# Induced-set attention with a maxout MLP: four block copies on GpSimd, one fp32 matmul later, another table of departures

## The chip, the cores and the metric

One Trainium2 chip, one core of it. The metric is the device time of one execution in microseconds (us); of several runs the median is taken.

## The reference

There are four batches of 12544 tokens with 128 channels, 32 inducing vectors, and a maxout MLP with 1024 hidden columns. Cut to what matters:

```python
def mab(q, kv):                       # scale = 1 / sqrt(128)
    s = scale * (q @ kv.transpose(0, 2, 1))
    a = np.exp(s - s.max(-1, keepdims=True))
    a /= a.sum(-1, keepdims=True) + 1e-09
    return a @ kv
h = mab(I, x)                         # 32 summary rows per batch
x = mab(x, h).reshape(B * N, 128)     # every token attends to the 32 rows
return np.maximum(x @ w1, x @ w2) @ w_out
```

## The kernel before

Each batch is 98 chunks of 128 tokens. The kernel works in two passes per batch. The first pass makes the 32 rows h: scores against the inducing vectors, exponentials, sums over tokens. The second pass never forms the attention output. As max(a, b) = a + max(0, b - a), the kernel applies the weights to h first: `hwd` is h times (w2 - w1), `m1` is h times w1 times w_out. For a token with exponentials e, the unnormalised result is relu(e hwd) w_out + e m1, and the division by the sum of e comes last, at the output.

The tokens of the second pass are cut into blocks of up to 16 chunks, four quarters of up to four chunks; a quarter's exponentials lie on 32 of the 128 partitions. These steps work on them:

- **Scores** (`stage`, L614): a column-tiled burst on TensorE of one block; ScalarE takes the exponentials (L633). Several blocks can follow one another in a burst.
- **Row phase** (`phase`, L1028): four row-tiled jobs side by side, each filling one PSUM bank. A job makes hidden columns from e and `hwd`, or opens an output group with e times `m1`. ScalarE (L1044) or VectorE (L1047) takes the relu of a bank.
- **Finals** (`final_one`, L840): matmuls of 128x128 that multiply relu tiles with w_out into an output group. VectorE scales a finished group (L867) and SyncE's queue stores it (L895).

In the first and last block some groups are "full": they aren't opened in a row phase. `linear_last` closes them (L817) with e on all 128 partitions times `m1bd`, a 128x4x128 tile that holds the q-th 32 rows of m1 in slot q and zeros elsewhere. GpSimd zeroes the tile once, at the start (L221).

The first pass of batch b + 1 is threaded into the second pass of batch b. `pool_accum` (column bursts, L384 and L403) sums over tokens; VectorE adds the parts into the tile `hacc` (L415 and L417). From `hacc` runs a chain of small steps. `small_rep` multiplies `hacc` by the fp32 tile `repd` (L429), so that h's sums stand four times over the partitions; VectorE takes the reciprocal (L432) and scales (L434). `small_h` transposes the result (L442, copied at L444). `small_hwd` makes `hwd` (L505, evicted at L508 and L511). `small_m1` makes m1 (L518), and VectorE casts it out of PSUM (L525 and L529), in batches 0 and 3 also blocks of it into `m1bd`, one instruction for each 32 partitions, ahead of m1 itself.

The order of all instructions is fixed while the program is built. A planner (`Clock`) keeps an estimated time for TensorE, ScalarE, VectorE and each PSUM bank, and at each step picks a row phase, a column burst, a final or a small step. `ready` says when a small step may go: `small_rep` as soon as the estimate says that `hacc` is written (`esrr`). The table `DEV` lists steps at which the planner departs from its own rule: 1 prefers finals, 2 a phase, 3 suppresses column work, 4 asks for column work early. On the chip semaphores keep the order right: an instruction whose input is late waits, and everything behind it on its engine waits too.

Of the kernel before, what the change touches and what calls it, by code (L numbers as in the profile page):

```python
# [16 lines left out]
INF = 1e9  # L17
# [85 lines left out]
def kernel(  # L103
# [9 lines left out]
    nc = tc.nc  # L113
    B, N, C = x.shape
# [27 lines left out]
    def bank(shape, dtype=F32, only=None):  # L142
        i = min(range(8), key=lambda j: ck.bank[j]) if only is None else only
        uid[0] += 1
        return i, psum.tile(shape, dtype, name=f"ps{uid[0]}", tag=f"bank{i}", bufs=1)
# [46 lines left out]
    m1bd = consts.tile([128, 4, C], F16, name="m1bd")  # L192
# [5 lines left out]
    with tc.manual_schedule(engines={ET.PE, ET.DVE, ET.Activation, ET.Pool, ET.SP}):  # L198
# [80 lines left out]
        def p1_esum(i):  # L279
            n = parts[0][i][1]  # L280
            et, ready = st[0]["et", i]
            ck.wait(ready, "p1")
            j = 0
            for m in pieces(n):
                nc.tensor.matmul(
                    out=st[0]["eps"][0 : m * M, 0:1],
                    lhsT=et[:, j : j + m, :].rearrange("p k m -> p (k m)"),
                    rhs=ones16[:, 0:1],
                    start=(summed["E"] == 0),
                    stop=(summed["E"] + m == K),  # L290
                    skip_group_check=True,
                )
                j += m
                summed["E"] += m
            st[0]["endE"] = ck.run(0.03 * len(pieces(n)))

        def p1_hsum(i, lo=0, hi=P1):
            n = parts[0][i][1]
            et, ready = st[0]["et", i]
            ck.wait(ready, "p1")  # L300
            for j in range(lo, min(hi, n)):
                nc.tensor.matmul(  # L302
                    out=st[0]["hps"][:, 0:M],
                    lhsT=xn_at[0, i][:, j, :],
                    rhs=et[:, j, :],
                    start=(summed["H"] == 0),
                    stop=(summed["H"] == K - 1),
                )
                summed["H"] += 1
            st[0]["end"] = ck.run(0.029 * (min(hi, n) - lo))  # L310
# [175 lines left out]
        def small_sums():  # L486
            es, ready = st[0]["es"]
            ps = st[0]["eps"]
            ck.wait(ready, "p1")
            nc.tensor.matmul(out=ps[:, 2:3], lhsT=rep32, rhs=es, start=True, stop=True, skip_group_check=True)  # L490
            end = ck.run(0.11)
            st[0]["rs"] = smp.tile([128, 1], F32, name="rs_0", tag="rs_")
            st[0]["rw"] = smp.tile([128, 1], F32, name="rw_0", tag="rw_")
            nc.vector.reciprocal(out=st[0]["rs"], in_=ps[:, 2:3])
            nc.vector.tensor_scalar(out=st[0]["rw"], in0=st[0]["rs"], scalar1=1.0 / scale, scalar2=None, op0=ALU.mult)
            ck.bank[st[0]["eb"]] = st[0]["rsr"] = ck.on_dve(end, 0.34)
# [18 lines left out]
        def small_m1(b):  # L515
            bi, ps = bank([128, 512])
            ck.wait(max(ck.bank[bi], st[b]["hT4r"]), "p1")
            nc.tensor.matmul(out=ps[:, 0:128], lhsT=st[b]["hT4"], rhs=w1out, start=True, stop=True)  # L518
            end = ck.run(0.06)
            m1 = smp.tile([128, C], F16, name=f"m1_{b}", tag="m1")  # L520
            bd = {0: [0], B - 1: [0, 1, 2, 3]}.get(b, [])
            outs = [(m1bd[32 * q : 32 * (q + 1), q, :], slice(32 * q, 32 * (q + 1))) for q in bd]
            for o, r in outs + [(m1, slice(0, 128))]:
                if b == 0:
                    nc.vector.tensor_scalar(  # L525
                        out=o, in0=ps[r, 0:128], scalar1=st[0]["rw"][r, :], scalar2=None, op0=ALU.mult
                    )
                else:
                    nc.vector.tensor_copy(out=o, in_=ps[r, 0:128])  # L529
                ck.bank[bi] = ck.on_dve(end, 0.2)  # L530
            st[b]["m1"] = m1
            st[b]["m1r"] = ck.bank[bi]

# [386 lines left out]
        def want_linear():  # L920
# [31 lines left out]
        }  # L952
        LIMIT = -16

# [107 lines left out]
        for b in range(1, B):  # L1062
            base = DONE0[b - 1]
            t_first, t_step = (6, 2.2) if b == 1 else (-6, 3.4)
            for u in range(NU):
                if b == 1:
                    s, turn, acc = 25 + 5 * u, 45 + 1.5 * u, 55 + 2 * u
                else:
                    s = turn = 13 + 8.2 * u
                    acc = s + 12  # L1070
                at(base + int(s), pool_scores, b, u)
                at(base + int(turn), pool_turn, b, u)
                if u % 2:
                    at(base + int(acc), pool_accum, b, u)
            s, end = int(s), base + int(acc)
            at(base + s + 2, pool_rest, b)
            at(end, small_rep, b)
            at(end, small_h, b)
            at(end, small_hwd, b)
            at(end, small_m1, b)  # L1080
            for j in range(14):
                at(base + int(t_first + t_step * j), transpose_x_dma, b, j)
# [8 lines left out]
        def ready(f, a):  # L1091

            if f in (weights_1, weights_1b):
                return True
            d = st[a[0]]
            now = ck.pe
            if f is pool_scores and a[1] >= NEU and ("eT", a[1] - NEU) not in d:
                return False
            if f is pool_turn and a[1] >= NEU and ("sum", a[1] - NEU) not in d:
                return False  # L1100
            if f is pool_scores:
                return d.get(("T", (U * a[1] + U - 1) // (P1 // 2)), INF) + (8.0 if a[0] == 1 else 10.0) <= now
            if f is pool_rest:
                return d.get(("T", 13), INF) + 6.0 <= now
            if f is pool_turn:
                return d.get(("eu", a[1]), (0, INF))[1] <= now
            if f is pool_accum:
                return d.get(("eT", a[1]), (0, INF))[1] + (9.5 if a[0] == 1 else 11.5) <= now and (a[1] < NU - 1 or "et" in d)
            if f is small_rep:
                return d.get("esrr", INF) <= now  # L1110
            if f is small_h:
                return d.get("haccr", INF) <= now
            if f in (small_hwd, small_m1):
                if f is small_m1 and a[0] == 0 and w_of["w1out"] > now:
                    return False
                return d.get("hT4r", INF) <= now
            return True

        COL = (pool_scores, pool_accum)
        FULL = (pool_rest, small_rep, small_h, small_hwd, small_m1)  # L1120

        def side_work():
# [83 lines left out]
        while state["g"] < len(groups) or held:  # L1206
# [19 lines left out]
            now = tp <= ck.pe + early or tp <= tf and tf > ck.pe  # L1226
            if how == 1 and tf < INF:
                now = False
            if how == 2 and tp <= ck.pe + 0.2:
                now = True  # L1230
# [47 lines left out]
```

## Time and profile before

| | |
|---|---|
| runs | 326.05, 326.20, 543.13 us; median 326.2 us |
| profiled execution | 325.93 us, span 324.1 us, granted TensorE clock 1.0 |
| TensorE matmuls | 317.5 us busy (98%), 5404 instructions |
| TensorE weight loads | 241.2 us (74%) |
| VectorE | 283.4 us (87%), 512 instructions |
| ScalarE | 280.1 us (86%), 558 instructions |
| GpSimd | 28.0 us (9%), 56 instructions |
| memory traffic | 167 GB/s over the span |

The span runs from the first to the last instruction of the profiled execution; its own time has 1.8 us more around it. PE is TensorE, DVE is VectorE, ACT is ScalarE, POOL is GpSimd, SP is SyncE. A row of the timeline gives the start, the duration, the engine, the line, the operation, the tiles (output <- inputs), the shapes and a count when equal instructions were merged; in brackets stands the idle time before it and what ended it. Matmuls overlap: their durations include the pipeline, so the distance between two starts tells more than a duration does. A row of the busy times in stretches gives the stretch, its length, and then the busy time of PE, PEld (weight loads), DVE, ACT and POOL.

### The profile page before, as it was taken

What the parts mean: (1) busy time and instruction counts of PE and PEld (TensorE: products, weight loads), DVE (VectorE), ACT (ScalarE), POOL (GpSimd) and SP (SyncE); (2) the same over time, 40 slices, a digit from 0 to 9 for tenths busy, and PEclk for the clock granted to TensorE, in tenths of its full rate; (3) what the DMA queues carried; (4) which work ended last, traced back from release to release, by engine and by line L of the source; (5) the groups of instructions that cost most, each with busy time, mean ns of one, the idle gap of its engine ahead of it and who ended that gap; (6) DMA issues with size and microseconds to landing.
All of it is one profiled execution on the core that took longest, in us unless ns stands there. A gap on an engine that the chain in (4) does not pass through costs nothing.

```text
span 324.1 us, 12585 instructions
## 1 busy us (share of the span) xinstructions
PE 317.5 (98%) x5404; PEld 241.2 (74%) x5404; DVE 283.4 (87%) x512; ACT 280.1 (86%) x558; POOL 28.0 (9%) x56
## 2 busy tenths in 40 slices
PE   7899999999999999999999999999999999999996
PEld 3786777777767777777777777777777777777786
DVE  2479999988989998999989989988989999999974
ACT  4679899998878999999988999998879999999860
POOL 7460000000450000000040000000000000000000
DMA  8999999965779999984279999783421322223233
GB/s 205 207 202 213 215 223 196 237 136 134 232 161 242 225 247 210 192 188 121 101 150 243 219 254 217 163 204 107 117 99 67 115 86 81 82 90 127 84 114 115
DMA packets 71895, 53.65 MB, mean 166 GB/s; under 512 B 52352, under 2 KB 57376, under 8 KB 71840
## 3 DMA queue, kind: packets, MB, share of 16 engines
q1 hardware_dynamic: 65232, 38.57, 48.6%
q0 software_dynamic: 6464, 14.22, 22.8%
q8 instruction: 42, 0.69, 0.8%
q14 instruction: 13, 0.11, 0.1%
q10 hardware_dynamic: 144, 0.07, 0.1%
HBM read 28.33 MB, written 25.69 MB: 167 GB/s over the span
## 4 chain that ended last, share of the span: by engine, by line
PE 93%; DMA 3%; ACT 1%; POOL 1%; DVE 1%; issue 1%; POOLq 0%; DVEq 0%; ACTq 0%
PE ps L840 61%; PE ps L1028 22%; DMA xn<-in_x_dram 3%; PE ps L614 2%; PE ps L384 2%; PE ps L328 1%; PE ps L234 1%; PE ps L673 1%; PE ps L257 1%; ACT relu L1044 1%; PE ps L302 1%; PE ps L797 0%; PE ps L429 0%; PE ps L505 0%; POOL xn L166 0%
## 5 line engine op out<-in xcount | busy, mean ns | idle before, releaser
L1044 ACT ACTIVATE relu<-ps 128x512 f16<-128x512 f32 x462 | 244.2, 605 | 25.0 <-PE ps L1028 16.6
L1047 DVE TENSOR_SCALAR relu<-ps 128x512 f16<-128x512 f32 x322 | 206.0, 683 | 16.0 <-PE ps L1028 14.5
L840 PE MATMUL ps<-woutp,relu 128*128 128x128 f16 x3136 | 217.5, 220 | 0.0
L840 PEld LDWEIGHTS <-relu 128*128 128x128 f16 x3136 | 176.6, 98 | 39.3 <-issue 29.0
L1028 PE MATMUL ps<-e,hwd 32*128 32x512 f16 (+2 forms) x888 | 88.6, 358 | 0.3 <-ACT e L633 0.3
L867 DVE TENSOR_TENSOR o<-ps,rp 128x512 f32<-128x512 f32 (+3 forms) x108 | 68.5, 634 | 6.3 <-PE ps L840 3.4
L1028 PEld LDWEIGHTS <-hwd 32*128 32x128 f16 x888 | 24.6, 91 | 21.2 <-issue 1.1
L1028 PE MATMUL ps<-m,e 32*128 32x128 f16 x381 | 38.9, 217 | 0.0
L1028 PEld LDWEIGHTS <-e 32*128 32x128 f16 x381 | 21.2, 92 | 3.2 <-issue 0.7
L166 POOL DMA_DIRECT2D xn<-in_x_dram x33 | 18.2, 563 | 6.2 <-DMA xn<-in_x_dram 3.8
L339 ACT ACTIVATE eu<-ps 128x512 f16<-128x512 f32 x18 | 10.9, 615 | 0.1
L633 ACT ACTIVATE e<-ps 128x512 f16<-128x512 f32 (+2 forms) x21 | 10.5, 571 | 0.2 <-PE ps L614 0.2
L245 DVE COPY xT<-ps 128x512 f16<-128x512 f16 (+3 forms) x12 | 5.6, 484 | 5.7 <-PE ps L234 5.2
L234 PE MATMUL ps<-identity,xn 128*128 128x128 f16 x98 | 8.1, 221 | 1.3 <-DMA xn<-in_x_dram 0.8
L614 PE MATMUL ps<-xT,hT 128*32 128x512 f16 (+3 forms) x114 | 8.4, 361 | 0.0
L248 ACT COPY xT<-ps 128x896 f16<-128x896 f16 (+3 forms) x9 | 5.4, 622 | 3.2 <-PE ps L234 3.1
L234 PEld LDWEIGHTS <-xn 128*128 128x128 f16 x98 | 5.7, 98 | 2.7 <-DMA xn<-in_x_dram 1.4
L328 PE MATMUL ps<-xT,inducingT 128*32 128x512 f16 x72 | 6.3, 384 | 0.0
L164 POOL COPY pace<-hacc 128x1 f32<-128x1 f32 x2 | 0.4, 183 | 68.5 <-DVE hacc L417 68.5
L273 ACT ACTIVATE et<-ps 128x224 f16<-128x224 f32 (+3 forms) x11 | 4.1, 407 | 1.9 <-PE ps L257 1.8
L614 PEld LDWEIGHTS <-hT 128*32 128x32 f16 x114 | 2.8, 94 | 3.6 <-issue 2.4
L384 PE MATMUL ps<-xn,eT 128*32 128x128 f16 x288 | 5.5, 220 | 0.0
(94 smaller groups left out, 105.1 us busy)
## 6 DMA issues: line engine op xcount, KB each, us to landing
out_dram<-o SPq DMA_DIRECT2D x85, 256.0 KB, 2.5
xn<-in_x_dram POOLq DMA_DIRECT2D x24, 448.0 KB, 11.7
out_dram<-o SPq DMA_DIRECT2D x20, 128.0 KB, 2.0
xn<-in_moe_w_dram POOLq DMA_DIRECT2D x4, 256.0 KB, 3.9
xn<-in_x_dram POOLq DMA_DIRECT2D x3, 224.0 KB, 8.8
xT<-xn SPq DMA_TRANSPOSE x42, 3.9
xf<-in_x_dram SPq DMA_DIRECT2D x1, 512.0 KB, 3.6
xf<-in_x_dram SPq DMA_DIRECT2D x1, 384.0 KB, 4.0
```

Source lines behind the costliest of these rows:

```text
L166: nc.gpsimd.dma_start(out=xn_at[b, i][lo:hi, 0:n, :], in_=xr[b, lo:hi, k0 : k0 + n, :])
L234: nc.tensor.transpose(ps[:, j, :], xn_at[0, i][:, g + j, :], identity16)
L328: nc.tensor.matmul(out=ps[32 * g : 32 * (g + 1), :], lhsT=inducingT, rhs=xT_tiles[b % 2][:, U * u + 4 * g : U * u + 4 * (g + 1), :], start ...
L339: nc.scalar.activation(out=eu, in_=ps, func=AF.Exp, scale=scale, accum_out=st[b]["es"][:, u : u + 1])
L384: nc.tensor.matmul(out=ps[32 * g : 32 * (g + 1), 0:128], lhsT=eT[:, j, 32 * g : 32 * (g + 1)], rhs=xn_of(b, U * v + 4 * g + j), start=(j = ...
L614: nc.tensor.matmul(out=ps[32 * q : 32 * (q + 1), 128 * t : 128 * (t + n)], lhsT=hq, rhs=xT[:, c : c + n, :], start=True, stop=True, tile_p ...
L633: nc.scalar.activation(out=blk.e2[:, lo:hi], in_=ps[:, lo:hi], func=AF.Exp, scale=st[0]["rs"] if blk.b == 0 else scale,)
L840: nc.tensor.matmul(out=g.ps[:, 128 * c : 128 * (c + 1)], lhsT=g.blk.relu[q][:, 128 * (jb * w4 + t) : 128 * (jb * w4 + t + 1)], rhs=woutp[: ...
L867: nc.vector.tensor_mul(osb[:, 0:n, :], g.ps[:, 0 : n * C].rearrange("p (s c) -> p s c", s=n), rp)
L1028: nc.tensor.matmul(**seq[i])
L1044: nc.scalar.activation(out=dst, in_=src, func=AF.Relu)
L1047: nc.vector.tensor_scalar(out=dst, in0=src, scalar1=0.0, scalar2=None, op0=ALU.max)
```

## The change

It has three parts. In batch 3, `small_m1` casts m1 from PSUM first, and the four blocks of `m1bd` are then copied by GpSimd from m1 in SBUF; VectorE's four casts from PSUM are gone. Batch 0 keeps its one block on VectorE. In the planner, `small_rep` may go only 0.3 us (by the planner's estimate) after `hacc`. And the table of departures has other entries: 674 and 1517 go; 650, 659, 1467, 1486, 1522, 1604, 1613 and 1614 come. Lines behind 531 move down by five in the changed kernel (L840 becomes L845, L1028 becomes L1033, L817 becomes L822).

```diff
-            bd = {0: [0], B - 1: [0, 1, 2, 3]}.get(b, [])
-            outs = [(m1bd[32 * q : 32 * (q + 1), q, :], slice(32 * q, 32 * (q + 1))) for q in bd]
-            for o, r in outs + [(m1, slice(0, 128))]:
+            outs = [(m1, slice(0, 128))]
+            if b == 0:
+                outs.insert(0, (m1bd[0:32, 0, :], slice(0, 32)))
+            for o, r in outs:
...
                 ck.bank[bi] = ck.on_dve(end, 0.2)
+            if b == B - 1:
+                for q in range(4):
+                    r = slice(32 * q, 32 * (q + 1))
+                    nc.gpsimd.tensor_copy(out=m1bd[r, q, :], in_=m1[r, :])
...
-            579: 4, 580: 1, 584: 1, 587: 2, 616: 2, 638: 1, 646: 2, 658: 1, 674: 4, 685: 1, 688: 2, 690: 1,
+            579: 4, 580: 1, 584: 1, 587: 2, 616: 2, 638: 1, 646: 2, 650: 2, 658: 1, 659: 1, 685: 1, 688: 2,
...
-            1, 1492: 1, 1496: 1, 1507: 1, 1517: 1, 1521: 1, 1547: 1, 1557: 1, 1558: 3, 1564: 1, 1569: 1,
+            3, 1407: 4, 1409: 1, 1413: 3, 1420: 1, 1434: 1, 1442: 1, 1451: 4, 1454: 1, 1461: 2, 1467: 2,
+            1476: 3, 1480: 1, 1486: 1, 1492: 1, 1496: 1, 1507: 1, 1521: 1, 1522: 2, 1547: 1, 1557: 1, 1558:
+            3, 1564: 1, 1569: 1, 1596: 1, 1604: 2, 1613: 4, 1614: 1, 1639: 4, 1680: 1, 1682: 1, 1696: 1,
...
             if f is small_rep:
-                return d.get("esrr", INF) <= now
+                return d.get("esrr", INF) + 0.3 <= now
```

18 rows, old and new, of the table DEV are left out of this document.

## The prediction

> **What bounds the kernel now.** I read four views in this order: busy times and the chain that ended last, both on the profile page; TensorE's waits between 26 and 310 us; the busy times in stretches; the timeline around the lines that the change touches.
>
> ```profile
> PE 317.5 (98%) x5404; PEld 241.2 (74%) x5404; DVE 283.4 (87%) x512; ACT 280.1 (86%) x558; POOL 28.0 (9%) x56
> PE 93%; DMA 3%; ACT 1%; POOL 1%; DVE 1%; issue 1%; POOLq 0%; DVEq 0%; ACTq 0%
> PE ps L1028 <- ACT e L633: 0.3, 1, 0.3
> core 0: us, PE busy (x) PEld busy (x) DVE busy (x) ACT busy (x) POOL busy (x), PEclk, DMA share, GB/s
> 243.00:248.00 5.00, 5.00 (x90) 3.88 (x87) 4.40 (x10) 4.55 (x10) 0.00 (x0) 1.00 0.14 52
> 243.00:310.00 67.00, 67.00 (x1103) 51.41 (x1101) 63.23 (x109) 61.80 (x120) 0.00 (x0) 1.00 0.25 92
> ```
>
> TensorE is busy 98% of the span and carries 93% of the chain. The third row is the whole answer for its waits from 26 to 310 us: 0.3 us, once. But a busy share can hide short stops, because overlapping matmuls cover the gap between two starts; so below I work with starts. In the last stretch, which the new order rewrites most, VectorE is busy 63.23 of 67.00 us and ScalarE 61.80. They empty the banks that TensorE fills, and have 4 to 5 us of slack between them and TensorE. So VectorE's work matters only if its delay uses up this slack; time that is freed there is worth nothing by itself.
>
> **Part 1: batch 3's m1.** Four VectorE casts from PSUM go, the cast of m1 itself comes first, and four GpSimd copies follow it.
>
> ```profile
> 243.15 1.19 DVE L529 CAST m1bd<-ps 32x128 f16<-32x128 f32 x4 [0.72 <-PE ps L518]
> 244.35 0.29 DVE L529 CAST m<-ps 128x128 f16<-128x128 f32 x1
> L164 POOL COPY pace<-hacc 128x1 f32<-128x1 f32 x2 | 0.4, 183 | 68.5 <-DVE hacc L417 68.5
> L546 POOL TENSOR_TENSOR w<-xn,xn 128x512 f16<-128x512 f32 x2 | 2.5, 1268 | 4.1 <-DMA xn<-in_moe_w_dram 4.1
> 162.73 4.01 POOL L166 DMA_DIRECT2D xn<-in_x_dram  x7 [0.36 <-PE ps L429]
> 317.89 0.39 PE L817 MATMUL ps<-m1bd,e 128*128 128x128 f16 x4
> ```
>
> VectorE gets 1.19 us back, and m1 is ready 1.19 us earlier. TensorE had no wait there, so I cost this at nothing; the cover is its own dense stream. No SBUF copy of 32x128 by GpSimd is in the trace. It lies between 0.18 us (the 128x1 copy) and 1.27 us (the two-input 128x512 subtraction); I take 0.25, near the copy, since it has a single input and a quarter of the columns. That makes 1.0 us for four (bounds 0.7 to 5.1), ending near 244.5, or at worst 248.6. Their reader in the last block starts at 317.89, so some 70 us hide them, and its new wait on GpSimd is long met. Nothing stands behind the copies in GpSimd's queue: its last transfers were issued by 166.74. Cost: 0.
>
> **Part 2: the fp32 matmul (L429) later.** It reads the sum hacc, which VectorE writes at L417. Per batch, the rows from the work before to the work after:
>
> ```profile
> L429 PEld LDWEIGHTS ps<-hacc,repd x6: 186/188/191, 89.9 to 238.3; 128*128 128x128 f32 x6
> 89.52 0.34 PE L840 MATMUL ps<-woutp,relu 128*128 128x128 f16 x3
> 89.53 0.29 DVE L417 TENSOR_TENSOR hacc<-ps,hacc 128x129 f32<-128x129 f32 x1
> 89.97 0.46 PE L429 MATMUL ps<-hacc,repd 128*128 128x129 f32 x2
> 90.27 1.06 PE L840 MATMUL ps<-woutp,relu 128*128 128x128 f16 x16
> 161.35 0.73 PE L840 MATMUL ps<-woutp,relu 128*128 128x128 f16 x10
> 161.76 0.29 DVE L417 TENSOR_TENSOR hacc<-ps,hacc 128x129 f32<-128x129 f32 x1
> 162.20 0.46 PE L429 MATMUL ps<-hacc,repd 128*128 128x129 f32 x2
> 237.74 0.29 DVE L417 TENSOR_TENSOR hacc<-ps,hacc 128x129 f32<-128x129 f32 x1 [0.16 <-PE ps L403]
> 237.92 0.34 PE L840 MATMUL ps<-woutp,relu 128*128 128x128 f16 x3
> 238.06 1.29 DVE L1047 TENSOR_SCALAR relu<-ps 128x512 f16<-128x512 f32 x2
> 238.18 0.46 PE L429 MATMUL ps<-hacc,repd 128*128 128x129 f32 x2
> 239.26 0.16 DVE L432 RECIPROCAL rec<-ps 128x1 f32<-128x1 f32 x1
> 239.46 0.35 DVE L434 TENSOR_SCALAR h<-ps,rec 128x128 f16<-128x128 f32 x1
> 239.97 0.22 PE L442 MATMUL ps<-identity,h 128*128 128x128 f16 x1
> ```
>
> Sixteen matmuls of L840 from 90.27 give their pitch: (1.06 - 0.22) / 15 = 0.056. So the last one before L429 starts at 89.63, 161.85 and 238.03, and L429 follows after 0.34, 0.35 and 0.15. In all three batches it starts 0.15 after hacc is finished (89.82, 162.05, 238.03): it waits for hacc, unseen by the busy share. Without a wait the step lies between one pitch, 0.056, and the shortest seen, 0.15; I take 0.15, because the fp32 weights alone load in 0.188.
>
> The two programs' instruction orders, side by side, give what stands ahead of L429. Batch 1: 11 + 8 matmuls of L840 in place of 12 + 3, four more, 0.22 us of work. The last starts at 89.85, L429 at 90.00 (89.97 at least): saved 0.19 (to 0.22). Batch 2: the column burst that makes hacc's input moves ahead of a row phase, and VectorE's sum ahead of a relu; with that phase and eight matmuls between, hacc is ready in time, and the saving is 0.35 - 0.15 = 0.20 (to 0.29). Batch 3: five more, 0.28 us, and L429 at 238.46, where it was already as good as late: saved 0.00 (to 0.09). Nor could more arrive: the reciprocal starts at 239.26, behind relus that end at 239.35 by their rows, and L442 waits for its product. Sum: 0.39 (0.39 to 0.60). Queued behind L429 are only matmuls of L840; the chain after it (reciprocal, h, L442) keeps its distance.
>
> **Part 3: the table.** TensorE's instructions are the same kinds and counts. There are 222 row phases in both, and every relu count per engine stays. But the last block's scores join the burst of the two blocks before: 27 column bursts in place of 28.
>
> ```profile
> 273.91 0.51 PE L614 MATMUL ps<-xT,hT 128*32 128x512 f16 x8
> 274.35 0.84 PE L840 MATMUL ps<-woutp,relu 128*128 128x128 f16 x12
> 291.35 0.41 PE L614 MATMUL ps<-xT,hT 128*32 128x512 f16 x6
> 291.69 0.84 PE L840 MATMUL ps<-woutp,relu 128*128 128x128 f16 x12
> 241.85 1.05 PE L614 MATMUL ps<-xT,hT 128*32 128x512 f16 x16
> 242.83 0.23 PE L840 MATMUL ps<-woutp,relu 128*128 128x128 f16 x1
> 274.00:278.00 4.00, 4.00 (x72) 3.00 (x72) 3.96 (x7) 3.92 (x8) 0.00 (x0) 1.00 0.17 68
> 274.00:290.00 16.00, 16.00 (x259) 12.07 (x259) 15.36 (x26) 15.12 (x29) 0.00 (x0) 1.00 0.22 85
> 292.52 0.65 ACT L633 ACTIVATE e<-ps 128x512 f16<-128x512 f32 x1
> ```
>
> A burst of one block costs 291.69 - 291.35 = 0.34; four blocks cost 0.98. So a block is (0.98 - 0.34) / 3 = 0.21 and the turn into the mode and out 0.13. One turn fewer saves 0.13 (bounds: 0, if another stop takes it, and 0.34, if the joined block runs wholly beside the others). Its exponential, 0.65 on ScalarE, moves some 17 us earlier.
>
> **Sum.** 0 + 0.39 + 0.13 = 0.5 us off the profiled execution's own 325.93 (span 324.1). The median shown, 326.2, lies 0.27 above that execution, so the forecast is 326.2 - 0.5 = **325.7 us**. Its own range: 325.3 (savings at their upper ends, 0.60 + 0.34) to 326.0.
>
> **Rivals.**
>
> *The change doesn't save what it says: 326.2.* The stops come back elsewhere, for hacc or at L442, and another wait takes the turn's 0.13. For it: each stop is only 0.2 us, and batch 3 already shows that L442 can hold the gain back. Against: after L429, TensorE meets nothing late in batches 1 and 2.
>
> *ScalarE becomes late at the joined burst: 326.3.* In 274 to 278 ScalarE is busy 3.92 of 4.00, with 0.08 for an exponential of 0.65. The relus behind it would be 0.57 late; if no bank is spare, TensorE stands for that long, and what 292 gives back on ScalarE doesn't return it. 0.57 - 0.52 = +0.05, or +0.65 at most with the savings gone (326.85). It decides once the delay outlasts the banks that TensorE has ready. Against: up to 290 ScalarE idles 16.00 - 15.12 = 0.88, enough to catch up.
>
> *GpSimd's copies hold up VectorE: up to 329.0.* If VectorE stood still during the four copies at their upper price, it would lose 5.1 us, where it gains 1.19 and has 5.00 - 4.40 = 0.6 idle in 243 to 248: TensorE would stop for 3.3 us, and 326.2 + 3.3 - 0.5 = 329.0. It decides from 1.8 us for the four. Against, GpSimd's subtraction beside two relus:
>
> ```profile
> 88.08 1.28 DVE L1047 TENSOR_SCALAR relu<-ps 128x512 f16<-128x512 f32 x2
> 88.16 1.27 POOL L546 TENSOR_TENSOR w<-xn,xn 128x512 f16<-128x512 f32 x1 [1.80 <-DMA xn<-in_moe_w_dram]
> ```
>
> Two relus took 1.28 beside it and 1.29 at 238.06 without it, so nothing was held. This rival is the headline rule of the Trainium skill, "SBUF — State Buffer", section "Who interferes with whom": VectorE and GpSimd share a port pair that one instruction locks whole. By the same section the lock needs a VectorE instruction in a two-port mode or with two SBUF inputs; VectorE's work here reads PSUM, and the trace's 1.28 agrees.
>
> **How the numbers follow.** Forecast 0.60, no saving 0.20, ScalarE late 0.13, VectorE held 0.05; 0.02 for causes I don't see. The range for 8 in 10 runs from 325.0 (325.3 less the 0.27 between execution and median) to 327.1 (326.85 plus 0.27); it covers the first three cases and little of the fourth. About 2%, 6.5 us, is what a measurement of this kernel can tell from no change. Not one case reaches it: faster would need thirteen times the sum, slower a stop of 0.15 at each of some 45 row phases. I leave 0.01 for faster and 0.03 for slower; 0.96 for within.
>
> **What would show it.** Right: L429 within about 0.15 of the last L840 before it in batches 1 and 2, one L614 burst of 14 near 274 lasting about 0.65, none at 291; the m1 cast at 243.2, copies of 0.2 to 0.3 us on GpSimd, relus beside them still 0.64 each. Wrong: a step before L1028 or L442 longer than before; relus at 243 to 249 stretched; new TensorE waits between 274 and 290. A change of more than 1 us either way would overturn the sum.

## The result and the profile after

The changed kernel takes 325.03 us (median), the kernel before 326.07 in the same sessions. The ratio is 0.9968, with a 95% interval of 0.9959 to 0.9977: 1.0 us or 0.3% faster, clear of noise, and within 2%. Two executions far above all others, 543 us of the kernel before and 1527 us in one experiment, count in no ratio. The forecast was 325.7 (325.0 to 327.1). The direction was right, the forecast gain of 0.5 was half of what came, and the forecast's own range of 325.3 to 326.0 missed the time.

The profiled execution's span is 323.2 us (before 324.1). Its busy and chain rows look as before, except that TensorE's 5404 matmuls are busy 0.9 us less; nothing in them tells where 1 us went:

```profile
PE 316.6 (98%) x5404; PEld 240.8 (75%) x5404; DVE 282.5 (87%) x508; ACT 280.0 (87%) x558; POOL 28.8 (9%) x60
PE 93%; DMA 3%; POOL 1%; ACT 1%; issue 0%; DVE 0%; POOLq 0%; ACTq 0%
```

The starts of matmuls tell. From the timeline of the changed kernel, the stretches around the fp32 matmul L429 in batches 1, 2 and 3, the joined burst of scores (L619, formerly L614), and batch 3's casts and copies:

```profile
89.58 0.62 PE L845 MATMUL ps<-woutp,relu 128*128 128x128 f16 x8
90.04 0.46 PE L429 MATMUL ps<-hacc,repd 128*128 128x129 f32 x2
91.18 0.22 PE L442 MATMUL ps<-identity,h 128*128 128x128 f16 x1
...
161.16 0.62 PE L845 MATMUL ps<-woutp,relu 128*128 128x128 f16 x8
161.62 0.44 PE L429 MATMUL ps<-hacc,repd 128*128 128x129 f32 x2
161.90 0.39 PE L845 MATMUL ps<-woutp,relu 128*128 128x128 f16 x4
...
237.43 0.62 PE L845 MATMUL ps<-woutp,relu 128*128 128x128 f16 x8
237.89 0.44 PE L429 MATMUL ps<-hacc,repd 128*128 128x129 f32 x2
238.96 0.35 DVE L434 TENSOR_SCALAR h<-ps,rec 128x128 f16<-128x128 f32 x1
239.38 0.22 PE L442 MATMUL ps<-identity,h 128*128 128x128 f16 x1
...
242.56 0.29 DVE L530 CAST m<-ps 128x128 f16<-128x128 f32 x1 [0.72 <-PE ps L518]
242.92 1.31 POOL L535 COPY m1bd<-m 32x128 f16<-32x128 f16 x4 [76.97 <-DVE m L530]
...
272.92 0.73 PE L619 MATMUL ps<-xT,hT 128*32 128x512 f16 x14
273.58 1.18 PE L845 MATMUL ps<-woutp,relu 128*128 128x128 f16 x18
```

In every batch L429 now starts about 0.06 after the matmul before it (161.16 + 7 x 0.056 = 161.56, then 161.62), where the gaps were 0.33, 0.33 and 0.13. The joined burst lasts 273.58 - 272.92 = 0.66, where two took 0.44 + 0.34.

Laying the starts of all 3136 finals of both kernels side by side gives a ledger. From the first final, which came 0.12 later in this execution, to the last, the changed kernel gains 1.13 us (the rows, each rounded, sum to 1.16):

| Place | forecast | measured |
|---|---|---|
| L429, batch 1 (gap 0.326 to 0.060) | 0.19 | 0.27 |
| L429, batch 2 (0.332 to 0.056) | 0.20 | 0.28 |
| L429, batch 3 (0.132 to 0.056) | 0.00 | 0.08 |
| start of the final behind L429, batches 2 and 3 | - | 0.04 |
| joined burst, less 0.03 in a row phase at 275.9 | 0.13 | 0.09 |
| row phase at 85.1 (0.39 to 0.33) | - | 0.06 |
| batch 3, from 239.5 to 246 | 0 | 0.34 |

The largest surprise is the last row. In the timeline of the kernel before it is one row phase, the second behind the matmul that makes batch 3's m1:

```profile
243.93 1.07 PE L840 MATMUL ps<-woutp,relu 128*128 128x128 f16 x16
244.56 0.68 DVE L867 TENSOR_TENSOR o<-ps,rp 128x512 f32<-128x512 f32 x1
244.93 0.39 PE L1028 MATMUL ps<-e,hwd 32*128 32x512 f16 x2
244.94 0.23 PE L1028 MATMUL ps<-m,e 32*128 32x128 f16 x1
245.30 0.37 PE L1028 MATMUL ps<-e,hwd 32*128 32x512 f16 x1
245.30 0.34 PE L1028 MATMUL ps<-m,e 32*128 32x128 f16 x3
245.60 0.84 PE L840 MATMUL ps<-woutp,relu 128*128 128x128 f16 x12
```

From the phase's first matmul to the next final pass 245.60 - 244.93 = 0.67 us, where the median of 222 phases is 0.33. Three of its four jobs start at once, the fourth only at 245.30, and with it the last three matmuls of the third. VectorE's eviction L867 ends at 245.24; it had stood in VectorE's queue behind the 1.48 us of casts. The planner's bank numbers, which the trace doesn't show, agree: this eviction empties bank 3, and the four jobs fill banks 6, 2, 5 and 3. What the runs have yet to show is that the casts weren't hidden: that they kept an output bank occupied which this phase needed.

### The profile page after: what moved, and what is told of

It reads as the page before. It is cut to its first block, busy times and chain, and to the rows that moved or that the text cites. A ratio compares the mean times of both kernels' runs of the same rounds, so it can differ in the third digit from the quotient of the medians.

```text
span 323.2 us, 12584 instructions
## 1 busy us (share of the span) xinstructions
PE 316.6 (98%) x5404; PEld 240.8 (75%) x5404; DVE 282.5 (87%) x508; ACT 280.0 (87%) x558; POOL 28.8 (9%) x60
## 4 chain that ended last, share of the span: by engine, by line
PE 93%; DMA 3%; POOL 1%; ACT 1%; issue 0%; DVE 0%; POOLq 0%; ACTq 0%
PE ps L845 61%; PE ps L1033 22%; DMA xn<-in_x_dram 3%; PE ps L619 2%; PE ps L384 2%; PE ps L328 1%; POOL xn L166 1%; PE ps L678 1%; ACT relu L1049 1%; PE ps L234 0%; PE ps L302 0%; PE ps L802 0%; PE ps L505 0%; PE ps L257 0%; PE ps L429 0%
## 5 line engine op out<-in xcount | busy, mean ns | idle before, releaser
L1052 DVE TENSOR_SCALAR relu<-ps 128x512 f16<-128x512 f32 x322 | 205.9, 682 | 16.3 <-PE ps L1033 14.8
L845 PE MATMUL ps<-woutp,relu 128*128 128x128 f16 x3136 | 217.4, 220 | 0.0
L845 PEld LDWEIGHTS <-relu 128*128 128x128 f16 x3136 | 176.6, 98 | 39.4 <-issue 29.1
L1033 PE MATMUL ps<-e,hwd 32*128 32x512 f16 (+2 forms) x888 | 88.2, 358 | 0.3 <-ACT e L638 0.3
L1033 PEld LDWEIGHTS <-hwd 32*128 32x128 f16 x888 | 24.5, 91 | 21.1 <-issue 1.1
L1033 PE MATMUL ps<-m,e 32*128 32x128 f16 x381 | 38.7, 217 | 0.0
L1033 PEld LDWEIGHTS <-e 32*128 32x128 f16 x381 | 21.2, 92 | 2.9 <-issue 0.4
L619 PE MATMUL ps<-xT,hT 128*32 128x512 f16 (+3 forms) x114 | 8.2, 361 | 0.0
L535 POOL COPY m1bd<-m 32x128 f16<-32x128 f16 x4 | 1.1, 284 | 77.1 <-DVE m L530 77.0
```

Source lines behind the costliest of these rows:

```text
L619: nc.tensor.matmul(out=ps[32 * q : 32 * (q + 1), 128 * t : 128 * (t + n)], lhsT=hq, rhs=xT[:, c : c + n, :], start=True, stop=True, tile_p ...
L845: nc.tensor.matmul(out=g.ps[:, 128 * c : 128 * (c + 1)], lhsT=g.blk.relu[q][:, 128 * (jb * w4 + t) : 128 * (jb * w4 + t + 1)], rhs=woutp[: ...
L1033: nc.tensor.matmul(**seq[i])
L1052: nc.vector.tensor_scalar(out=dst, in0=src, scalar1=0.0, scalar2=None, op0=ALU.max)
```

## The experiments

Unless something else is said, each kernel keeps the instruction order of its parent on every engine: the planner's estimates are fed as in the parent, and only what is emitted changes. The diffs are shortened. Added lines move the numbers behind them: in the rows below the cast L529 stands at L529 to L536, finals (L840) at L840 to L853, the eviction L867 at L867 to L873, row phases (L1028) at L1028 to L1034, and VectorE's relu (L1047) at L1052.

**Copies alone, in the old order.** The edit to the kernel before:

```diff
-            for o, r in outs + [(m1, slice(0, 128))]:
+            for o, r in [(m1, slice(0, 128))]:          # batch 3
                 nc.vector.tensor_copy(out=o, in_=ps[r, 0:128])
+            for q in range(4):
+                r = slice(32 * q, 32 * (q + 1))
+                nc.gpsimd.tensor_copy(out=m1bd[r, q, :], in_=m1[r, :])
```

> The kernel before, with every TensorE, ScalarE and SyncE instruction in its old order; only batch 3's four casts into m1bd leave VectorE and follow as GpSimd copies from m1. Theory (VectorE's casts cost TensorE time: the output eviction L867 stood behind them, freed its bank at 245.24, and the row phase at 244.93 stood until 245.30): that phase falls from 0.665 to 0.33 us, and the time from 326.07 by 0.34 to about 325.7. Rival (the gain there came from the new order; VectorE's casts were hidden, as the prediction had it): the phase keeps about 0.66, no change.

It took 325.72 us, ratio 0.9990 (0.9980 to 0.9999): 0.3 us faster. The profile comes from a second run of the same kernel:

> Again the kernel before in its old order with batch 3's casts turned into GpSimd copies, for its profile. Theory: the row phase near 244.9 takes 0.33 us (0.665 before) and the eviction of VectorE ahead of it ends 1.19 us earlier; span 323.8. Rival: the phase keeps 0.66.

Its timeline:

```profile
243.74 0.69 DVE L873 TENSOR_TENSOR o<-ps,rp 128x512 f32<-128x512 f32 x1 [0.27 <-PE ps L846]
244.97 0.39 PE L1034 MATMUL ps<-e,hwd 32*128 32x512 f16 x1
245.30 0.84 PE L846 MATMUL ps<-woutp,relu 128*128 128x128 f16 x12
```

The eviction now ends at 244.43, before the phase starts; all four jobs start at 244.97, and the phase takes 0.33. So the casts had cost 0.34, and the order had no part in it. The span was 323.9.

**m1 first, casts after it, all on VectorE.**

```diff
-            for o, r in outs + [(m1, slice(0, 128))]:
+            for o, r in [(m1, slice(0, 128))] + outs:   # batch 3
```

> The kernel before in its old order; VectorE casts batch 3's m1 first and then makes the four casts into m1bd from PSUM as before. Theory (the queue on VectorE matters: the eviction stands behind all five casts whatever their order): the row phase at 244.9 stays at 0.66 us, span 324.1, no change. Rival (m1 itself was late, 1.19 us behind the four casts): the phase falls to 0.33 and the span to 323.8.

```profile
245.46 0.69 DVE L867 TENSOR_TENSOR o<-ps,rp 128x512 f32<-128x512 f32 x1
245.83 0.39 PE L1028 MATMUL ps<-e,hwd 32*128 32x512 f16 x2
246.20 0.37 PE L1028 MATMUL ps<-e,hwd 32*128 32x512 f16 x1
246.51 0.68 PE L840 MATMUL ps<-woutp,relu 128*128 128x128 f16 x9
```

This execution reached its first final 0.9 us later than the kernel before (25.72 against 24.83), which shifts all its times and lengthens its span to 325.1; from the first final to the last both take 296.2. The phase still takes 0.68, and its fourth job again follows the end of the eviction (246.15) by 0.05. So m1's lateness isn't the cause; VectorE's queue is.

**The new order alone.** The changed kernel, with batch 3's blocks cast by VectorE again:

```diff
-                    nc.gpsimd.tensor_copy(out=m1bd[r, q, :], in_=m1[r, :])
+                    outs.insert(0, (m1bd[r, q, :], r))  # cast from PSUM, ahead of m1
```

> The changed kernel with its own order on every other engine; batch 3's four blocks of m1bd are again cast from PSUM by VectorE ahead of m1, and GpSimd copies nothing. Theory (casts ahead of relus and an eviction on VectorE stop TensorE): 1.19 us of casts, less the 0.47 us that VectorE stood idle there, make VectorE 0.7 late at 243.3, and the row phases between 244 and 247 lose 0.3 to 0.7 us: 325.03 becomes 325.3 to 325.7. Rival (with the new order the casts are hidden, and the order alone brought all of the gain): no change, 325.0.

326.06 us, ratio 0.9998 (0.9989 to 1.0008): the whole gain is gone, more than I had expected to lose. In its view of waits, and then its timeline:

```profile
PE ps L1034 <- DVE m L536: 0.8, 1, 0.8
242.39 1.19 DVE L536 CAST m1bd<-ps 32x128 f16<-32x128 f32 x4 [0.72 <-PE ps L518]
242.74 0.38 PE L1034 MATMUL ps<-e,hwd 32*128 32x512 f16 x1
243.59 0.29 DVE L536 CAST m<-ps 128x128 f16<-128x128 f32 x1
243.94 0.37 PE L1034 MATMUL ps<-e,hwd 32*128 32x512 f16 x1 [0.82 <-DVE m L536]
244.24 0.96 PE L846 MATMUL ps<-woutp,relu 128*128 128x128 f16 x14
```

In this order the phase right behind m1 waits for the cast of m1: 244.24 - 242.74 = 1.50 in place of 0.33. The same casts that cost 0.34 in the old order cost 1.17 in the new one. What is it waiting for, the values or the bank?

**The new order, m1 first, casts after it on VectorE.**

```diff
-                    outs.insert(0, (m1bd[r, q, :], r))
+                    outs.append((m1bd[r, q, :], r))
```

> The changed kernel's order, nothing on GpSimd: VectorE casts m1 first and then the four blocks from the same PSUM bank. Theory (the row phase behind m1 takes over the bank of m1's matmul, and every cast that reads this bank holds it): the stop of 1.17 us in that phase stays as with the casts ahead of m1, phase 1.5 us, span 324.2. Rival (the phase waits for m1's values): the phase falls to 0.33 and the span to 323.2.

```profile
PE ps L1034 <- DVE m1bd L536: 0.7, 1, 0.7
242.90 1.18 DVE L536 CAST m1bd<-ps 32x128 f16<-32x128 f32 x4
243.03 0.38 PE L1034 MATMUL ps<-e,hwd 32*128 32x512 f16 x1
244.13 0.37 PE L1034 MATMUL ps<-e,hwd 32*128 32x512 f16 x1 [0.71 <-DVE m1bd L536]
244.43 0.96 PE L846 MATMUL ps<-woutp,relu 128*128 128x128 f16 x14
```

The phase takes 1.40; it waits for the last cast into `m1bd`, which it never reads. So it waits for the bank of m1's matmul. The planner's numbers agree: m1's matmul fills bank 4, and the phase behind it fills banks 2, 1, 6 and 4. With the copies on GpSimd, which read m1 in SBUF, that bank is free after one cast. The span was 324.4.

**L429 later, all else old.** The matmul is emitted a number of finals later than the planner had it: five in batches 1 and 3, two in batch 2.

```diff
-            nc.tensor.matmul(out=ps[:, 0 : C + 1], lhsT=repd, rhs=st[b]["hacc"], start=True, stop=True)
+            later.append([{1: 5, 2: 2, 3: 5}[b], emit])  # emit: this matmul, reciprocal and scaling
```

> The kernel before, all else in its order; only the fp32 matmul L429 is issued five matmuls of L840 later in batch 1, two in batch 2 (a row phase follows there) and five in batch 3. Theory (L429 stood waiting for hacc; without a wait it starts 0.056 after the matmul before it): the gaps ahead of it fall from 0.326 to about 0.06, from 0.332 to about 0.22 and from 0.132 to 0.056, and with 0.02 less behind it the time falls by 0.5 us to about 325.6. Rival (what the prediction had: a step of 0.15 at least and nothing in batch 3): 0.18 + 0.11 + 0 = 0.29, about 325.8. Rival (the waits come back at L442): no change.

325.88 us, ratio 0.9995 (0.9985 to 1.0004), a gain of 0.15 that the interval doesn't tell from none, and less than any expectation but the last. From the first final to the last it is 0.17 shorter. Its timeline in batch 1 (L434 is the fp32 matmul, L448 the transpose):

```profile
90.05 0.45 PE L434 MATMUL ps<-hacc,repd 128*128 128x129 f32 x2
90.33 0.78 PE L846 MATMUL ps<-woutp,relu 128*128 128x128 f16 x11
91.15 0.23 PE L448 MATMUL ps<-identity,h 128*128 128x128 f16 x1
```

The gap ahead of L429 is 0.056, but the transpose now starts 91.15 - (90.33 + 10 x 0.056) = 0.26 after the last final, 0.20 more than its 0.056 before. In batch 2 the gaps are 0.22 ahead of L429 and 0.155 ahead of the transpose. The stop had moved to L442. Batch 3 kept its gain: the transpose's gap stayed at 0.056.

**L429 and the transpose later.**

```diff
-            nc.tensor.transpose(ps[:, 0:128], st[b]["h4"], identity16)
+            later.append([{1: 4, 2: 3}[b], emit])        # emit: the transpose and its copy
```

> The kernel before in its old order, but L429 is issued five, two and five matmuls of L840 later in batches 1, 2 and 3, and the transpose L442 four later in batch 1 and three later in batch 2. Theory (the chain hacc, L429, reciprocal, h, L442 has a fixed length on VectorE; work must stand both ahead of L429 and behind it): the gaps ahead of L442 return from 0.255 and 0.155 to 0.056, and the time falls by 0.27 + 0.11 + 0.09 = 0.47 to about 325.6, against 325.88 with L429 alone moved. Rival (the wait moves on once more, to the copy of h or L505): 325.88 as with L429 alone.

325.63 us, ratio 0.9981 (0.9967 to 0.9996). In its timeline (L434 and L451):

```profile
90.16 0.45 PE L434 MATMUL ps<-hacc,repd 128*128 128x129 f32 x2
90.45 1.00 PE L853 MATMUL ps<-woutp,relu 128*128 128x128 f16 x15
91.28 0.22 PE L451 MATMUL ps<-identity,h 128*128 128x128 f16 x1
```

91.28 - (90.45 + 14 x 0.056) = 0.05: in batch 1 both stops are gone, in batch 2 the transpose's; 0.22 stays ahead of L429 there, where a row phase left no more finals to put in front. The time fell by 0.45 us.

**Both gains in the old order.** The two edits of the run before and the copies together:

```diff
+            later.append([{1: 5, 2: 2, 3: 5}[b], emit])  # L429
+            later.append([{1: 4, 2: 3}[b], emit])        # L442
+                    nc.gpsimd.tensor_copy(out=m1bd[r, q, :], in_=m1[r, :])
```

> The kernel before in its old order, with L429 and L442 moved as in the run that moved both, and batch 3's four blocks copied by GpSimd. Theory (the two gains are separate stops and add): 326.05 - 0.45 - 0.34 = 325.26; what is left to 325.0 is the table's (the joined burst 0.12, batch 2's swap of burst and phase 0.17). Rival (one of them only moves the stop): 325.6.

325.12 us, ratio 0.9976 (0.9967 to 0.9986) against a median before of 325.92 in that session: 0.8 us, the sum of 0.45 and 0.34. The gains are separate and add.

**The old table with the new rule.** Here the order changes, and so do the planner's steps:

```diff
-            579: 4, 580: 1, 584: 1, 587: 2, 616: 2, 638: 1, 646: 2, 650: 2, 658: 1, 659: 1, 685: 1, 688: 2,
+            579: 4, 580: 1, 584: 1, 587: 2, 616: 2, 638: 1, 646: 2, 658: 1, 674: 4, 685: 1, 688: 2, 690: 1,
...
```

> The changed kernel with the table of departures of the kernel before; the 0.3 us in the rule for L429 and the GpSimd copies stay. The planner then makes another order behind batch 1: 28 column bursts in place of 27, 222 row phases as before. Theory (the gains are single stops; the table brings the joined burst and lets the rest of the order close up without new stops): 325.1 to 325.4. Rival (the entries are tied to the steps that they were set for, and a shifted order meets new stops): above 325.6.

325.30 us, ratio 0.9986 (0.9972 to 1.0001). In its starts the gaps ahead of L429 and L442 are 0.056 to 0.066 and the phase behind m1 is short; no new stop above 0.06 us appears, so the rival falls. The profiled span was 323.6 (its other executions 323.2 to 325.3), 0.4 more than with the new table: the second burst and the phase at 85.1 (0.39) account for 0.15, the rest I did not trace.

**Six times the copies.**

```diff
-                for q in range(4):
+                for q in [0, 1, 2, 3] * 6:
```

> The changed kernel, GpSimd makes its four copies six times over (24 copies, same data). Theory (GpSimd's copies and VectorE's work on PSUM do not hold each other): 24 copies of 0.28 to 0.33 us run from 242.9 to about 250.8, the relus of VectorE beside them stay at 0.64 us each in pairs and the time stays at 325.0. Rival (GpSimd holds VectorE during a copy): VectorE loses up to 6.8 us in 8, TensorE stops, 327 to 331.

324.95 us, ratio 0.9967 (0.9953 to 0.9982), as the changed kernel. GpSimd's row, and VectorE's beside it; the last row is the changed kernel's own:

```profile
242.93 8.11 POOL L535 COPY m1bd<-m 32x128 f16<-32x128 f16 x24 [76.97 <-DVE m L530]
245.14 1.33 DVE L1052 TENSOR_SCALAR relu<-ps 128x512 f16<-128x512 f32 x2
250.52 1.89 DVE L1052 TENSOR_SCALAR relu<-ps 128x512 f16<-128x512 f32 x3
...
245.13 1.33 DVE L1052 TENSOR_SCALAR relu<-ps 128x512 f16<-128x512 f32 x2
```

24 copies fill 8.1 us of GpSimd, and VectorE's relus neither stretch nor shift (by more than 0.01 us).

**Batch 0's block on GpSimd as well.**

```diff
-                outs.insert(0, (m1bd[0:32, 0, :], slice(0, 32)))
+            if b in (0, B - 1):                          # GpSimd copies block 0, or all four
```

> The changed kernel in its own order; batch 0's one block of m1bd is also copied by GpSimd from m1, so VectorE loses its 0.25 us cast at 26.0 us. Theory (a cast taken from VectorE is worth only what TensorE stood for it; here VectorE is idle 0.20 us behind it and the row phase at 26.26 waits for ScalarE's exponential): no change, 325.0. Rival (every cast taken from VectorE shortens the time by its own duration): 324.8.

324.97 us, ratio 0.9971 (0.9956 to 0.9986): the changed kernel's time. VectorE's rows in this run, and last the changed kernel's own:

```profile
25.99 0.26 DVE L526 TENSOR_SCALAR m<-ps,rw 128x128 f16<-128x128 f32 x1
26.69 1.89 DVE L1052 TENSOR_SCALAR relu<-ps 128x512 f16<-128x512 f32 x3 [0.44 <-PE ps L1033]
...
26.73 1.89 DVE L1052 TENSOR_SCALAR relu<-ps 128x512 f16<-128x512 f32 x3 [0.20 <-PE ps L1033]
```

The cast of 0.25 us that left VectorE turned into idle time (0.44 in place of 0.20). A cast is worth what TensorE stood for it: 0 here, 0.34 in batch 3's old order, 1.17 in the new one. None of these versions beats the changed kernel clearly.

## Why the prediction was right or wrong

**Part 1 failed** at "TensorE had no wait there, so I cost this at nothing; the cover is its own dense stream". The prediction itself warned that a busy share hides short stops, and then measured starts only around L429. Starts inside row phases would have shown 0.67 beside a median of 0.33. It also said that VectorE's work matters only when its delay uses up some 4 to 5 us of slack in 243 to 310; but slack over 67 us says nothing of a bank that is needed 0.4 us after its eviction starts. The two orders with the casts left on VectorE show both sides: 0.34 and 1.17. What the copies take was near (0.28 each and 1.31 for the four, forecast 0.25 and 1.0), and their 70 us of cover was right.

**Part 2 was right in mechanism**: L429 waited for `hacc` in all three batches, unseen by the waits. The mis-sized term is the step without a wait. I took 0.15, because the fp32 weights load in 0.188; it is 0.056 to 0.066 in the runs that removed the wait, so that load doesn't add to the step. That is 0.08 in each of the three batches, the whole difference between 0.39 and 0.63. In batch 3 the claim that L442 would hold the gain back failed: its gap was 0.056 before, no wait, and h was finished 0.16 ahead of it before (239.46 + 0.35 to 239.97) and 0.07 after (238.96 + 0.35 to 239.38): that slack took the gain. "The chain after it keeps its distance" holds only because the planner moves L442 with L429. With L429 alone moved, the rival came true in batches 1 and 2: 0.27 saved in front of L429 in batch 1, 0.20 paid again at L442.

**Part 3** was near: one turn fewer measured 0.12 for 0.13, less 0.03. The 0.06 at 85.1 wasn't in the sum; the old table still has that longer phase (0.39), so the gain comes with the new table, but what held the phase isn't shown.

**The rivals.** ScalarE late at the joined burst: one phase of 0.36 at 275.9, 0.03 in place of up to 0.57; what held that phase isn't shown. VectorE held by GpSimd: refuted for this work with 24 copies; the finer conditions of the Trainium skill, "SBUF — State Buffer", section "Who interferes with whom", fit, as VectorE's work beside them reads PSUM and its relus stayed at 1.33 for two. No saving: refuted, though a change of the table and the rule alone, without the copies, gave just that (326.06).

The measured time lies at the low edge of the range, and that it lies inside is luck. The sum was 0.52 with an upper end of 0.94, and 1.04 came; the prediction's own mark, that a change of more than 1 us would overturn the sum, was passed. The range holds 325.03 only because 0.27, the distance between one execution and the median, was taken off its low end. A further 0.13 of the miss in the time is its base: the forecast started from 326.2, and the kernel before then measured 326.07. That the change stays within 2% was safe, because no case came near 6.5 us.

## What to carry to other kernels

Where the busiest engine is busy 98%, read the distances between its starts at every place that an edit touches, and compare each with the median of its kind; the list of waits showed 0.3 us here where about 1.0 was to be had. Time taken from a helper engine is worth what the bottleneck stood for it: look for what waits in that engine's queue behind the removed work, and which buffer it holds. When one step of a dependent chain is moved later to hide a wait, move the step at the chain's end with it, or the wait goes there.

## What the runs showed of the hardware

An fp32 matmul of 128x129 started 0.056 us after an f16 matmul, although its weights load in 0.19. GpSimd copied 32x128 f16 in 0.28 us, one every 0.34, with no effect on VectorE's relus, which read PSUM. The matmuls of one row phase wait in order: the job whose bank was still occupied held up the remaining matmuls of the others too, 0.34 to 1.17 us at a time, and the list of waits named it in the longer cases alone.
